# Second product of an MLP by Strassen's seven half-size products, in pairs of tiles, on one Trainium2 core

## Chip, core and metric

The program runs on one core of one Trainium2 chip. The metric is device time in microseconds (us), the median over runs of the whole program. The engines are named as in the profile: PE (matrix products), PEld (its weight loads), DVE (vector), ACT (scalar), POOL (general purpose; it also issues the loads of q, k, v and the weights), SP (issues the DMA transposes).

## What is computed

Inputs are q, k, v of shape 4 x 8 x 768 x 64 (batch, heads, positions, head size), a gain `g_ln` of 512, and two weight matrices. The reference, cut to what matters:

```python
gamma = 1.0 - 2.0 ** (-5.0 - np.arange(H))            # one decay per head
for t in range(S):
    state = gamma * state + outer(k[:, :, t], v[:, :, t])
    y[:, :, t] = scale * (q[:, :, t] @ state)
x = y with the 8 heads side by side                    # 4 x 768 x 512
xn = (x - mu) / np.sqrt(var + 1e-06) * g_ln            # per position, over 512
out = x + np.maximum(xn @ w_ch1, 0.0) @ w_ch2          # 512 -> 2048 -> 512
```

The output is 4 x 768 x 512 in fp32.

## The kernel before

**Tiles.** The 4 x 768 positions are 24 tiles of 128 positions. Tiles 0 to 3 are the first chunk of each of the four batches, tiles 4 to 23 the other five chunks of each batch, batch after batch. Products are in bf16 with fp32 sums in PSUM.

**Steps of a tile.** Each step is one short function, called by its name (line numbers are those of the profile):

- `k`, `q`, `v` (L334): POOL issues the loads, which turn fp32 into bf16. `gk`, `gq`, `gv` (L363): a one-element copy on POOL that waits for a load.
- `tr` (L377): SP issues a DMA transpose of q and k. `eq` (L383): DVE scales the transposed q into `trq`.
- `vis` (L392, L398), a *visit*: PE multiplies k by q for the tile, or from tile 8 on for a pair of tiles (8 and 9, 10 and 11, ... 22 and 23) into banks X0 to X3, and q by the state of the chunk before into banks Y0 and Y1.
- `am` (L405): DVE multiplies with the decay mask into `asb`, two instructions per tile. `py` (L420): PE adds `asb` times v in Y0 and Y1. Y then holds x of the tile.
- `vg` (L454): POOL scales v. `pd` (L462): PE adds k times the scaled v to the running state in bank PD. `pb` (L472): DVE writes the state out as bf16, two instructions.
- `bn` (L428, L429): DVE takes mean and variance. `xn` (L438): DVE makes (x - mean) times gain in bf16, two instructions. `xc` (L444): ACT copies x to `x_all`.
- `ex` (L492): for tiles 8 and later SP issues a DMA transpose of `xn` into `xnt`.
- `m` (L517): PE multiplies with the first weight matrix `w1`, in groups of 1, 2 or 4 tiles (128, 256 or 512 columns per instruction; groups 0 to 7 are tiles 0 to 7, groups 8 to 11 are tiles 8 to 15 in twos, groups 12 and 13 tiles 16 to 19 and 20 to 23). A call fills one bank with 512 columns. `r` (L528, L530): ACT, at times DVE, takes the positive part into `h1`, 128 x 16 x 512 for four tiles.
- `z` (L540): PE multiplies `h1` of one tile with the second weight matrix `w2`: 16 instructions of 512 columns, in four calls. For tile 23 they are cut into 384 and 128 columns.
- `sq` (L505, ACT) and `rs` (L510, DVE): one over the standard deviation, in `rstd`. Since it is positive, it is applied only at the end: `ad` (L547): DVE takes `z`'s result times `rstd` plus x into `osb` (fp32). `st` (L554): ACT issues the store.

**Order.** The order of all steps is a table of names written out in the file (`ORDER`, some 1,000 entries); each engine runs its own instructions strictly in that order, and waits by semaphores where it needs another engine's result. After a `/` a name has the engine or the PSUM banks: `r8_4/A`, `z8_0//M`. Between a tile's visit and its first product, and between its first and its second, the table puts work of other tiles.

## Time and profile before

| what | number |
|---|---|
| runs | 211.12, 211.79 and 214.57 us, median 211.79 |
| span of the profiled execution, first to last instruction | 208.5 us |
| granted PE clock | 1.000 |
| PE busy | 203.1 us in 2031 instructions |
| DVE busy | 126.0 us in 297 instructions |
| ACT busy | 76.8 us in 168 |
| POOL busy | 95.6 us in 145 |
| DMA | 27.11 MB in 109946 packets |

Of the profiled execution only the span is given; it is 3.3 us below the median of the runs. To read the profile: a row by line gives the operation, its output and inputs by the program's names, the shape, how often it occurs, the busy time of the group and the mean length of one in ns. Matmuls are pipelined, so one of them lasts longer than the distance to the next: the distance is read from the chain of work that ended last, where the length of a piece divided by its count is the pitch. In the timeline, `x2` means that neighbours on one line are merged, and the bracket says how long the engine was idle before and for whom. In a table of windows, the first number is the length of the stretch, then come the busy times of the engines, the granted clock, the DMA share (over 1 where packets of several queues wait at once) and GB/s.

### The profile page before, as it was taken

Reading aid. Unit: us, or ns where it says so; the run is one execution under the profiler, and the core shown is the slowest. Engines: PE = TensorE matmul, PEld = TensorE weight load, DVE = VectorE, ACT = ScalarE, POOL = GpSimd, SP = SyncE. Lnnn points to the kernel's source line nnn. Section 1 sums busy time; section 2 is a strip of 40 time slices with the busy share of each in tenths; the row PEclk is TensorE's granted clock in tenths of the full one; section 3 lists DMA queues with packets and bytes.
Section 4 is the critical chain, followed back from the end, with each engine's and each line's share of the span. In section 5 each row is a group of like instructions: output and inputs, shape, how many; then the busy total and the mean of one; then the engine's idle time right before and its main releaser. Section 6 shows DMA issues by size and latency. Waiting matters only on the chain.

```text
span 208.5 us, 4986 instructions
## 1 busy us (share of the span) xinstructions
PE 203.1 (97%) x2031; PEld 131.4 (63%) x2031; DVE 126.0 (60%) x297; ACT 76.8 (37%) x168; POOL 95.6 (46%) x145
## 2 busy tenths in 40 slices
PE   7999999999999999999999999999999999999994
PEld 3568999897558566676587686565545444444443
DVE  7687898696349858579695666888948303110023
ACT  6466644442400414415137124223372612346000
POOL 8997593793696788770687559300000000000000
PEclk9999999999999999999999999999999999999999
DMA  9999999999999999999999999965032400015005
GB/s 129 175 180 181 160 199 163 167 183 155 150 140 159 129 180 144 161 98 207 205 160 161 203 161 116 159 79 129 0 105 101 102 0 3 0 50 203 0 3 201
DMA packets 109946, 27.11 MB, mean 130 GB/s; under 512 B 102625, under 2 KB 106977, under 8 KB 109922
## 3 DMA queue, kind: packets, MB, share of 16 engines
q0 software_dynamic: 77024, 13.37, 84.9%
q1 hardware_dynamic: 28242, 6.85, 24.4%
q10 hardware_dynamic: 4656, 6.56, 9.6%
q8 instruction: 16, 0.26, 0.6%
q14 instruction: 8, 0.07, 0.1%
HBM read 27.30 MB, written 6.29 MB: 161 GB/s over the span
## 4 chain that ended last, share of the span: by engine, by line
PE 92%; DVE 4%; DMA 2%; issue 0%; ACTq 0%; ACT 0%; DVEq 0%
PE X L517 40%; PE M L540 27%; PE Y L540 10%; PE PD L540 4%; PE X L392 3%; PE Y L420 3%; PE PD L462 2%; DMA osb<-in_q_dram 2%; DVE asb L405 1%; PE Y L398 1%; DVE trq L383 1%; DVE xn L438 1%; DVE bns L428 1%; PE Y L369 1%; PE M L369 1%; PE X L325 1%
## 5 line engine op out<-in xcount | busy, mean ns | idle before, releaser
L517 PE MATMUL X<-xnt,w 128*128 128x128 bf16 (+2 forms) x896 | 93.8, 257 | 0.0
L528 ACT ACTIVATE h<-X 128x512 bf16<-128x512 f32 x89 | 51.2, 602 | 81.7 <-PE X L517 70.9
L517 PEld LDWEIGHTS <-w 128*128 128x128 bf16 x896 | 66.1, 98 | 20.5 <-issue 0.2
L540 PE MATMUL M<-w,h 128*128 128x512 bf16 x256 | 61.5, 379 | 0.0
L540 PEld LDWEIGHTS <-h 128*128 128x128 bf16 x400 | 37.4, 98 | 37.9
L405 DVE TENSOR_TENSOR asb<-X,mask 128x512 bf16<-128x512 f32 x48 | 30.5, 682 | 12.3 <-PE X L392 12.1
L454 POOL TENSOR_TENSOR vg<-v,vsc 128x512 bf16<-128x512 bf16 x20 | 21.2, 1062 | 7.9 <-DMA v<-in_v_dram 7.8
L547 DVE SCALAR_TENSOR_TENSOR osb<-M,rstd,x_all 128x512 f32<-128x512 f32 x16 | 11.9, 746 | 20.6 <-PE M L540 20.2
L334 POOL DMA_DIRECT2D v<-in_v_dram x24 | 21.8, 911 | 3.7 <-DMA w<-in_moe_w_ch_dram 2.0
L444 ACT CAST x_all<-Y 128x256 bf16<-128x256 f32 (+1 forms) x39 | 14.4, 411 | 24.7 <-DVE xn L438 24.7
L540 PE MATMUL Y<-w,h 128*128 128x512 bf16 (+1 forms) x96 | 21.8, 370 | 0.0
L428 DVE BATCH_NORM_STATS2 bns<-Y 128x6 f32<-128x256 f32 (+1 forms) x39 | 16.3, 453 | 8.5 <-PE Y L420 8.3
L438 DVE SCALAR_TENSOR_TENSOR xn<-Y,mv,gb 128x256 bf16<-128x256 f32 (+1 forms) x39 | 18.6, 512 | 1.2 <-PE Y L420 0.6
L472 DVE TENSOR_TENSOR state<-PD,gch 64x256 bf16<-64x256 f32 x40 | 16.6, 415 | 0.6 <-PE PD L462 0.3
L334 POOL DMA_DIRECT2D qk<-in_q_dram x17 | 15.2, 893 | 1.3 <-issue 1.3
L334 POOL DMA_DIRECT2D qk<-in_k_dram x17 | 15.3, 898 | 0.9 <-issue 0.7
L547 DVE SCALAR_TENSOR_TENSOR osb<-PD,rstd,x_all 128x512 f32<-128x512 f32 (+1 forms) x3 | 1.9, 617 | 20.1 <-PE PD L540 20.1
L383 DVE TENSOR_TENSOR trq<-tr,qsc 128x512 bf16<-128x512 bf16 x17 | 9.1, 537 | 3.5 <-DMA tr<-qk 3.3
L561 PE MATMUL PD<-zeros 128*128 128x512 bf16 (+1 forms) x33 | 8.5, 392 | 1.2 <-DVE zeros L247 1.2
L420 PEld LDWEIGHTS <-asb 128*128 128x128 bf16 x192 | 8.0, 98 | 2.6 <-DVE asb L405 0.7
L363 POOL COPY scrap<-qk 1x1 bf16<-1x1 bf16 x28 | 4.9, 177 | 9.7 <-DMA qk<-in_k_dram 8.5
L540 PE MATMUL PD<-w,h 128*128 128x512 bf16 (+1 forms) x48 | 8.8, 326 | 0.0
(75 smaller groups left out, 130.5 us busy)
## 6 DMA issues: line engine op xcount, KB each, us to landing
out_dram<-osb ACTq DMA_DIRECT2D x23, 256.0 KB, 2.4
w<-in_moe_w_ch_dram POOLq DMA_DIRECT2D x8, 512.0 KB, 8.4
v<-in_v_dram POOLq DMA_DIRECT2D x24, 128.0 KB, 6.5
qk<-in_k_dram POOLq DMA_DIRECT2D x17, 128.0 KB, 6.8
qk<-in_q_dram POOLq DMA_DIRECT2D x17, 128.0 KB, 5.1
k<-in_k_dram POOLq DMA_DIRECT2D x6, 128.0 KB, 7.6
q<-in_q_dram POOLq DMA_DIRECT2D x6, 128.0 KB, 7.4
tr<-qk SPq DMA_TRANSPOSE x17, 6.1
```

What stands on the lines that cost most here:

```text
L334: nc.gpsimd.dma_start(out=dst, in_=tok[kind][TILES[t]])
L405: nc.vector.tensor_tensor(out=slot(asb, t)[:, :, par, :], in0=bank(("pa", t, par)).rearrange("p (i t) -> p i t", t=P), in1=mask.rearrange( ...
L420: nc.tensor.matmul(dst, lhsT=slot(asb, t)[:, h // 2, h % 2, :], rhs=v_of(t)[:, h, :], start=(not late and n == H and h == 0), stop=(h >= H ...
L428: nc.vector.bn_stats(out=bns[:, t, i, :], in_=x)
L438: nc.vector.scalar_tensor_tensor(out=dst, in0=src, scalar=mv[:, t, 0:1], in1=g, op0=ALU.subtract, op1=ALU.mult)
L444: nc.scalar.copy(out=dst, in_=src)
L454: nc.gpsimd.tensor_tensor(out=slot(vgs, chunk(t)), in0=v_of(t), in1=vsc[:, c, :].unsqueeze(2).to_broadcast([P, H, D]), op=ALU.mult)
L472: nc.vector.tensor_tensor(out=slot(state, chunk(t) - 1)[o, :, o], in0=pd[o, :, o], in1=gch[o, c - 1, :].unsqueeze(2).to_broadcast([D, NPAI ...
L517: nc.tensor.matmul(bank(("mm", g, ho))[:, j * n * P:(j + 1) * n * P], lhsT=w1[:, ko, (ho + j) * P:(ho + j + 1) * P], rhs=x[:, x0:x0 + n, k ...
L528: nc.scalar.activation(out=dst, in_=src, func=AF.Relu)
L540: nc.tensor.matmul(bank(("m2", t, piece))[:, 0:hi - lo], lhsT=slot(h1, t // 4)[:, ho, t % 4 * P:(t % 4 + 1) * P], rhs=w2[:, ho, lo:hi], st ...
L547: nc.vector.scalar_tensor_tensor(out=slot(osb, t + piece)[:, 0:hi - lo], in0=bank(("m2", t, piece))[:, 0:hi - lo], scalar=rstd[:, t:t + 1] ...
```

## The change

For tiles 0 to 7 nothing changes except places in memory. For tiles 8 to 23 the second product is made for two tiles together, by Strassen's scheme. With h of tile t and of tile t+1 cut into halves along the 2048 (h(t,0), h(t,1)) and `w2` cut into four blocks W11, T3 (upper right), W21, W22 of 1024 x 256, a pair needs seven products of 8 instructions with 256 columns (`s`, L607), where the two tiles took 32 instructions with 512 columns.

- `tm` (L582): DVE makes four sums of blocks of `w2` once (T1 = T3 - W11, T2 = W22 + T1, T3 = W22 + T3 in place, T4 = W21 - T2), each 128 x 2048 in bf16. T1, T2 and T4 lie in a new tile `early`, which first holds q, k, v and transposed k of early tiles.
- `sa` (L596): DVE makes four differences of halves of h per pair, each 128 x 1024 in bf16 (S1, S2, S4 in three shared tiles `sum`; the third one in place in `h1`).
- `o` (L621): DVE puts the products and x together in `osb`, six instructions per pair: the first with 512 columns (two blocks at once), five with 256. Six of the seven products are summed by PE in the two halves of one bank (`sm`), which `o` reads in between; the seventh has a bank of its own (`sb`). `ad` is left for tiles 0 to 7 only.
- Products of two tiles can be mixed only if both are normalized. For tiles 8 to 23, `sr` (L564, ACT) and `rt` (L568, DVE) make `rstd` per tile right after `bn`; `xn` writes fp32 (into `arg` and `grow`, which are free by then); and a new step `xg` (L572, ACT) multiplies by `rstd` and writes the bf16 `xn` that `ex` transposes.
- `xnt` has 3 slots for 4; `osb` has 3 slots of two tiles for 6 of one. Tile 23 is no longer cut 384/128 at the end; its two halves of 256 columns are stored apart.
- The table `ORDER` is the same up to the visit of tiles 8 and 9, and new from there on.

The diff, cut to its core:

```diff
 ORDER = """
...
-z2_3 ad0 tr10 gq10 z3_0//M v12 gk11 st0/A ad2 z3_1 tr11 eq8 q13 vis8//X2,X1,X3,X0 z3_2 am8b am8a
-gv10 vg10/ gv11 z3_3 am9a am9b py8 m7_12//X1 bn8 m7_4//X3 ad3 q12 py9 pd9 bn9 gk12 k13 m6_4//X0
+z2_3 ad0 tr10 gq10 z3_0//M v12 gk11 st0/A ad2 z3_1 tr11 eq8 q13 vis8//X2,X1,X3,X0 tm1 z3_2 am8b am8a
+z3_3 q12 am9a py8 am9b m6_4//X1 gk12 vg10/ bn8 py9 m7_8//X0 k13 xc9b xc8b bn9 sq7 vg11/ m7_4//X2
...
+    early = sb.tile([P, 12, DM], BF16, name="early")
...
-    osb = slots("osb", [P, DM], FP32)
+    osb = slots("osb", [P, 2, DM], FP32)
+    sums = [sb.tile([P, HK, P], BF16, name=f"sum{i}") for i in range(3)]
+    xhat = [arg.rearrange("p i t -> p (i t)"), grow]
...
-        dst, src, g = y_parts(t, half, slot(xns, t))
+        dst, src, g = y_parts(t, half, slot(xns if t < S0 else xhat, t))
...
+    @on("sr")
+    def _(eng, t):
+        nc.scalar.activation(out=rstd[:, t:t + 1], in_=mv[:, t, 1:2], func=AF.Sqrt, bias=epsb, scale=1.0)
+
+    @on("rt")
+    def _(eng, t):
+        nc.vector.reciprocal(out=rstd[:, t:t + 1], in_=rstd[:, t:t + 1])
+
+    @on("xg")
+    def _(eng, t):
+        nc.scalar.activation(out=slot(xns, t), in_=slot(xhat, t), func=AF.Copy, scale=rstd[:, t:t + 1])
+
+    W11, W21, W22, T3 = w2[:, 0:HK, 0:HM], w2[:, HK:, 0:HM], w2[:, HK:, HM:], w2[:, 0:HK, HM:]
+    T1, T2, T4 = (early_b[:, i * HK:(i + 1) * HK] for i in range(3))
+    S1, S2, S4 = sums
+
+    @on("tm")
+    def _(eng, i):
+        out, in0, in1, op = {1: (T1, T3, W11, ALU.subtract), 2: (T2, W22, T1, ALU.add),
+                             3: (T3, W22, T3, ALU.add), 4: (T4, W21, T2, ALU.subtract)}[i]
+        nc.vector.tensor_tensor(out=out, in0=in0, in1=in1, op=op)
...
+    def left(t, i):
+        return {1: h_of(t, 0), 2: h_of(t, 1), 3: S4, 4: h_of(t + 1, 1), 5: S1, 6: S2, 7: h_of(t + 1, 0)}[i]
+
+    right = {1: W11, 2: W21, 3: W22, 4: T4, 5: T1, 6: T2, 7: T3}
+
+    @on("sa")
+    def _(eng, t, i):
+        out, in0, in1 = {1: (S1, h_of(t + 1, 0), h_of(t + 1, 1)), 2: (S2, h_of(t, 0), S1),
+                         3: (h_of(t + 1, 0), h_of(t + 1, 0), h_of(t, 0)), 4: (S4, h_of(t, 1), S2)}[i]
+        {"P": nc.gpsimd, "": nc.vector}[eng].tensor_tensor(out=out, in0=in0, in1=in1, op=ALU.subtract)
...
+    @on("s")
+    def _(eng, t, i):
+        for ho in range(HK):
+            nc.tensor.matmul(product(t, i), lhsT=left(t, i)[:, ho, :], rhs=right[i][:, ho, :],
+                             start=(ho == 0 and i in (1, 2)), stop=(ho == HK - 1), skip_group_check=True)
+
+    @on("o")
+    def _(eng, t, i):
...
+            n, s, j, add = {2: (0, low, 2, o), 3: (0, high, 6, x), 4: (0, high, 3, o), 5: (1, high, 7, o),
+                            6: (1, low, 4, x)}[i]
+            out, in0, in1 = o[:, n, s], product(t, j), add[:, n, s]
+        nc.vector.tensor_tensor(out=out, in0=in0, in1=in1, op=ALU.add)
```

**How the table moves instructions.** Three places follow; the numbers in the names are those of buffers.

DVE from the visit of tiles 12 and 13 to the means of the first of the two, before (`trq` is scaled q, `asb` the masked product, `osb` the output tile):

```order
L405 TENSOR_TENSOR asb0_146<-X2_63,mask_74 128x4x128
L405 TENSOR_TENSOR asb1_147<-X1_62,mask_74 128x4x128
L405 TENSOR_TENSOR asb1_147<-X0_61,mask_74 128x4x128
L405 TENSOR_TENSOR asb0_146<-X3_64,mask_74 128x4x128
L472 TENSOR_TENSOR state1_96<-PD_68,gch_81 64x4x64 x2
L547 SCALAR_TENSOR_TENSOR osb1_159<-M_67,rstd_90,x_all_94 128x512
L428 BN_STATS bns_88<-Y0_65 128x6
L428 BN_STATS bns_88<-Y1_66 128x6
L429 BN_AGGR mv_89<-bns_88 128x2
```

The same engine in the change, from the end of the normalization of tile 12 past the visit of tiles 14 and 15 (`arg` is one of the two fp32 tiles for normalized x, `h10` is `h1` of tiles 8 to 11, `sum0` is S1):

```order
L451 SCALAR_TENSOR_TENSOR arg_79<-Y0_65,mv_89,gb_87 128x4x64
L582 TENSOR_TENSOR early_98<-w2_93,early_98 128x2048
L596 TENSOR_TENSOR sum0_149<-h10_144 128x1024
L568 RECIPROCAL rstd_90<-rstd_90 128x1
L418 TENSOR_TENSOR asb1_136<-X2_63,mask_74 128x4x128
L418 TENSOR_TENSOR asb0_135<-X0_61,mask_74 128x4x128
L418 TENSOR_TENSOR asb0_135<-X1_62,mask_74 128x4x128
L418 TENSOR_TENSOR asb1_136<-X3_64,mask_74 128x4x128
L553 SCALAR_TENSOR_TENSOR osb0_146<-M_67,rstd_90,x_all_94 128x512
L582 TENSOR_TENSOR w2_93<-w2_93 128x8x256
L596 TENSOR_TENSOR sum1_150<-h10_144,sum0_149 128x1024
L441 BN_STATS bns_88<-Y0_65 128x6
```

Between a visit's four `asb` instructions and the steps around them now stand two sums of `w2` and two of h, which were nowhere before; the reciprocal of tile 13 stands ahead of the `asb` rows.

SP around the transposes of tiles 8 to 15, before (rows with `tr` are q and k of a tile, rows with `xnt` are normalized x; the first two are x of tiles 8 and 9, the next two q and k of tiles 12 and 13, then x of tiles 10 and 11, then q and k of tiles 14 and 15):

```order
L492 DMA_TRANSPOSE xnt2_154<-xn0_148 128x4x128
L492 DMA_TRANSPOSE xnt2_154<-xn1_149 128x4x128
L377 DMA_TRANSPOSE tr5_135<-qk5_127 128x8x128
L377 DMA_TRANSPOSE tr0_130<-qk6_128 128x8x128
L492 DMA_TRANSPOSE xnt2_154<-xn2_150 128x4x128
L492 DMA_TRANSPOSE xnt2_154<-xn3_151 128x4x128
L377 DMA_TRANSPOSE tr1_131<-qk7_129 128x8x128
L377 DMA_TRANSPOSE tr2_132<-qk0_122 128x8x128
```

The same in the change:

```order
L505 DMA_TRANSPOSE xnt2_143<-xn0_137 128x4x128
L505 DMA_TRANSPOSE xnt2_143<-xn1_138 128x4x128
L390 DMA_TRANSPOSE tr0_122<-qk6_120 128x8x128
L390 DMA_TRANSPOSE tr5_127<-qk5_119 128x8x128
L390 DMA_TRANSPOSE tr2_124<-qk0_114 128x8x128
L390 DMA_TRANSPOSE tr1_123<-qk7_121 128x8x128
L505 DMA_TRANSPOSE xnt2_143<-xn3_140 128x4x128
L505 DMA_TRANSPOSE xnt2_143<-xn2_139 128x4x128
```

Tiles 12 and 13 have changed places, and the transposes of q and k of tiles 14 and 15 now stand ahead of those of x of tiles 10 and 11.

The end of ACT's queue, the last stores, before:

```order
L554 DMA out_0_dram<-osb2_160 128x512
L554 DMA out_0_dram<-osb4_162 128x512
L554 DMA out_0_dram<-osb3_161 128x512
L554 DMA out_0_dram<-osb5_163 128x384
L554 DMA out_0_dram<-osb0_158 128x128
```

And in the change, from the store of tile 18 on:

```order
L560 DMA out_0_dram<-osb0_146 128x512 x2
L560 DMA out_0_dram<-osb1_147 128x512
L560 DMA out_0_dram<-osb2_148 128x256
L560 DMA out_0_dram<-osb2_148 128x512
L560 DMA out_0_dram<-osb1_147 128x512
L560 DMA out_0_dram<-osb2_148 128x256
```

Before, tiles 20, 22 and 21 and the two pieces of tile 23 were left for the end; in the change it is tiles 18, 19 and 20, one half of tile 23, tiles 22 and 21, and the other half of tile 23.

171 lines of the change are left out of this document (95 added, 76 removed).

## The prediction

> **What bounds the kernel now.** I read the page first: engines, slices, and the chain that ended last.
>
> ```profile
> span 208.5 us, 4986 instructions
> PE 203.1 (97%) x2031; PEld 131.4 (63%) x2031; DVE 126.0 (60%) x297; ACT 76.8 (37%) x168; POOL 95.6 (46%) x145
> PE   7999999999999999999999999999999999999994
> DVE  7687898696349858579695666888948303110023
> DMA  9999999999999999999999999965032400015005
> GB/s 129 175 180 181 160 199 163 167 183 155 150 140 159 129 180 144 161 98 207 205 160 161 203 161 116 159 79 129 0 105 101 102 0 3 0 50 203 0 3 201
> PE 92%; DVE 4%; DMA 2%; issue 0%; ACTq 0%; ACT 0%; DVEq 0%
> ```
>
> PE is busy in every slice but the first and the last, and the chain is 92% PE. DVE is full only until about two thirds of the span and then nearly idle. DMA is full for 25 of the 40 slices. A busy PE may still hide gaps, since matmuls are pipelined, so I took the pitch from the pieces of the chain:
>
> ```profile
> 105.97 1.75 PE X L517 x16
> 198.42 3.45 PE PD L540 x16
> 204.68 0.91 PE PD L540 x16
> 205.61 0.35 DVE osb L547
> ```
>
> Instructions of 512 columns follow each other at 3.45/16 = 0.216 us, those of 256 columns (groups 8 to 11 on L517) at 1.75/16 = 0.109 us, half of it. Pieces of L517 and L540 come at this pitch from about 20 us to the end, so PE has no gaps to give: only less PE work, or a shorter end, can make the program faster, and every new wait of PE is added to its time.
>
> **Term 1, PE work.** The change removes 16 tiles x 16 = 256 instructions of 512 columns: 256 x 0.216 = 55.2 us. It adds 8 pairs x 7 x 8 = 448 of 256 columns: 448 x 0.109 = 49.0 us. No other PE work changes. Term: -6.2 us. The new products load weights of the same size from the same kind of tile at the pace at which groups 8 to 11 already do.
>
> [...]
>
> **Term 2, the end.** Before, the last matmul runs to 205.6, then come one short DVE instruction (0.35 us), the store of a strip of 64 KB and the closing. Stores cannot go faster than this:
>
> ```profile
> 190.00:192.00 2.00, 2.00 (x11) 0.89 (x10) 0.00 (x0) 1.09 (x2) 0.00 (x0) 1.00 1.00 378
> 202.69 3.65 ACTq L554 DMA_DIRECT2D out_dram<-osb  x5
> out_dram<-osb ACTq DMA_DIRECT2D x23, 256.0 KB, 2.4
> out_dram<-osb ACTq DMA_DIRECT2D x1, 64.0 KB, 1.6
> ```
>
> With a DMA share of 1.00 they move 378 GB/s, 0.69 us for a tile of 256 KB. In the new order the stores of tiles 19, 20, 22, 21 and both halves of 23 are issued around the last three calls of PE: 4 x 256 + 2 x 128 KB = 1.3 MB, issued in about 2.3 us, which take 3.5 us to move. The last one is behind a queue of about 0.8 us, and the last DVE instruction has 256 columns for 128 (0.1 us more). Term: +0.9 us. Lower bound +0.2 (if the stores keep up, the wider last piece alone), upper +1.3 (if they start 0.4 us later than I count).
>
> **Term 3, DVE from the visit of tiles 8 and 9 to that of 22 and 23.** This is where the new work lies. Visit to visit, before:
>
> ```profile
> 61.50:74.70 13.20, 13.20 (x159) 8.70 (x160) 9.74 (x22) 3.62 (x10) 9.99 (x19) 1.00 1.96 154
> 74.70:88.00 13.30, 13.30 (x139) 9.22 (x140) 9.90 (x25) 4.93 (x12) 10.66 (x18) 1.00 1.58 156
> 88.00:101.10 13.10, 13.10 (x135) 9.01 (x136) 9.71 (x22) 4.76 (x11) 5.18 (x12) 1.00 1.76 169
> 101.10:115.90 14.80, 14.80 (x153) 10.93 (x152) 10.16 (x25) 6.36 (x13) 10.94 (x16) 1.00 1.63 172
> 115.90:132.50 16.60, 16.60 (x159) 11.37 (x160) 11.34 (x22) 5.72 (x13) 12.83 (x19) 1.00 1.57 164
> 132.50:143.60 11.10, 11.10 (x111) 6.75 (x110) 9.06 (x21) 3.06 (x8) 0.00 (x0) 1.00 0.87 108
> 143.60:155.80 12.20, 12.20 (x107) 6.27 (x108) 8.97 (x22) 5.56 (x12) 0.00 (x0) 1.00 0.28 66
> 155.80:205.40 49.60, 49.60 (x289) 23.98 (x288) 12.51 (x24) 14.30 (x29) 0.00 (x0) 1.00 0.18 63
> ```
>
> The first seven rows: 94.3 us of PE, 68.9 us of DVE. In the same stretch the new order has 32 calls of `z` fewer (18 for 50, 0.863 us each), 21 calls of `s` (0.875 us each) and one more of `m`: 94.3 - 27.6 + 18.4 + 0.9 = 86.0 us of PE. For DVE it has 4 `tm`, 15 `sa`, 16 `o` (3 of them wide), 13 `rt`, and 7 `ad` and 5 `rs` fewer. Their prices:
>
> ```profile
> L300 DVE TENSOR_TENSOR mask<-vsc,cm 128x1024 f32<-128x1024 f32 x1 | 1.2, 1224 | 0.1
> L276 DVE TENSOR_TENSOR arg<-fidx,lgq 128x512 f32<-128x512 f32 x1 | 0.7, 673 | 0.0
> L383 DVE TENSOR_TENSOR trq<-tr,qsc x17: 404/426/2181, 44.0 to 149.8; 128x512 bf16<-128x512 bf16 x17
> L472 DVE TENSOR_TENSOR state<-PD,gch 64x256 bf16<-64x256 f32 x40 | 16.6, 415 | 0.6 <-PE PD L462 0.3
> L547 DVE SCALAR_TENSOR_TENSOR osb<-M,rstd,x_all 128x512 f32<-128x512 f32 x16 | 11.9, 746 | 20.6 <-PE M L540 20.2
> L510 DVE RECIPROCAL rstd<-rstd 128x1 f32<-128x1 f32 x8 | 1.0, 141 | 0.0
> ```
>
> The two fp32 rows give 0.12 us fixed and 1.08 ns per element; the bf16 row (median 426) then 0.60 ns per element. An `sa` (1024 elements, all bf16) is an estimate of 0.73 us by the bf16 row, 1.22 by the fp32 row; a `tm` (2048) 1.34 or 2.33. I take the bf16 prices, the operands being of its kind. An `o` reads PSUM like `state`: 0.42 us, the wide one 0.67. Sum: 68.9 + 4 x 1.34 + 15 x 0.73 + 13 x 0.42 + 3 x 0.67 + 13 x 0.14 - 7 x 0.75 - 5 x 0.14 = 88.6 us. That overstates, since back to back an instruction starts before the one ahead ends:
>
> ```profile
> 88.42 2.48 DVE L405 TENSOR_TENSOR asb<-X,mask 128x512 bf16<-128x512 f32 x4 [2.40 <-PE X L392]
> 128.62 2.18 DVE L383 TENSOR_TENSOR trq<-tr,qsc 128x512 bf16<-128x512 bf16 x1
> 128.48 2.03 POOL L454 TENSOR_TENSOR vg<-v,vsc 128x512 bf16<-128x512 bf16 x2
> ```
>
> Four `asb` of 0.68 us take 2.48 us: 0.08 us less each. With 48 instructions added that is up to 3.8 us: 84.8 us of DVE against 86.0 of PE, where it was 69 against 94. DVE is 99 to 103% loaded in this stretch and becomes nearly a second bound; behind each late DVE instruction are queued the `asb` rows of the next visit, and PE waits for them in `py`. After the last visit DVE has 12.5 us plus 17 `sa`, 32 `o` less 10 `ad`, about 32 us against 51.6 of PE: no bound there.
>
> The other two rows show a collision: a DVE instruction with two SBUF inputs, begun during POOL's `vg`, lasted until the second `vg` had ended, 2.18 us for 0.43. The new `sa` and `tm` are of that kind, and 13 `vg` lie in the stretch. I take 0.9 us of new PE waits for DVE, between 0 (if all fits) and 3 (88.6 - 86.0 and a collision not hidden).
>
> **Term 4, DMA transposes.** Here `xg` is the added link: after `bn` the chain to `m` runs over ACT and DVE (`sr`, `rt`, `xg`) and then to SP.
>
> ```profile
> 69.20 2.52 SPq L492 DMA_TRANSPOSE xnt<-xn  x2
> 71.82 4.18 SPq L377 DMA_TRANSPOSE tr<-qk  x2
> DMA to landing us min/median/max: 3.0/6.1/9.2
> 74.67 0.62 PE L392 MATMUL X<-trq,tr 64*128 64x128 bf16 x16
> 76.56 1.91 PE L517 MATMUL X<-xnt,w 128*128 128x256 bf16 x16
> ```
>
> SP issues x of tiles 8 and 9 at 69.2 and 70.5, then q and k of tiles 12 and 13 at about 71.8 and 73.6. `xg` puts these some 1.1 us later: one ACT instruction of 0.6 and the `pb` that now stands ahead of `xn`. The first product of tiles 8 and 9, which PE began at 76.6, is due at about 77.6 in the new order; that fits. Between the visits of tiles 8 and 10, and of 10 and 12, the new table has six calls of `z` and four of `m` (5.2 and 3.5 us), a visit of 0.9 and about 1.1 of `py` and `pd`: 21.3 us. So the visit of tiles 12 and 13 is due at 82.8 where it was 88.0, 5.2 us earlier, while its transposes are issued later: 73.6 + 1.1 + 1.4 of issue + 6.1 to land (the median for `tr`) + 0.4 for `trq` gives 82.6 us, with a spread of 3 us either way by the same row. As DMA is full there, I take 0.9 us; bounds 0 and 3.5. Next in SP's queue stand q and k of tiles 14 and 15, which wait for their loads, ahead of x of tiles 10 and 11; the same lateness passes on, rather than being paid again. Later loads have time, since the last visits come 8 us earlier, but the loads of tiles 21 to 23 stand at least 7 us of PE earlier in the table. `xg` itself costs ACT 16 x 0.6 us of idle time it has (ACT is 37% busy); if it were the bound, that would be 9.6 us.
>
> **Sum.** 208.5 - 6.2 + 0.9 + 0.9 + 0.9 = 205.0 us of span, 3.5 us less. The median of the runs, 211.79, is 3.3 us above the span; taken off that, 208.3 us.
>
> **Rivals.**
>
> - *Clean.* DVE and DMA keep up; new waits stay under 1.1 us in sum. For it: the prices of term 3 are upper ones, and PE had no gap after 20 us before. Against it: the loads of 99% on DVE and full DMA together. -6.2 + 0.9 + 0.3: 206.8 us, and faster by over 2% wherever waits stay under 1.1. Chance 0.34.
> - *DMA holds the visits.* The three intervals after the first pair's visit shrink from 39.6 to 32.5 us of PE while their DMA share is already 1.58 to 1.96. If loads and transposes cannot go faster, PE waits most of the 7.1 us; with 1.6 of it as slack, 5.5: -6.2 + 0.9 + 5.5 = +0.2, 212.0 us. Against it: GB/s there (154 to 169) is under the 203 to 207 of other slices. Chance 0.12.
> - *DVE holds PE, slower than before.* If `sa` and `tm` run at the fp32 price, they cost 15 x 0.49 + 4 x 0.99 = 11.3 us more, DVE has 96 to 100 us in a stretch of 86, and PE waits 10 to 14: -6.2 + 0.9 + 11.5 = +6.2, 218.0 us. It decides once DVE's work there passes 95 us. Chance 0.09. [...]
> - *Half-width matmuls do not pay half.* If the fixed part of an instruction were not hidden in the new stream, lengths would count instead of pitches:
>
> ```profile
> L540 PE MATMUL M<-w,h 128*128 128x512 bf16 x256 | 61.5, 379 | 0.0
> L517 PE MATMUL X<-xnt,w 128*128 128x256 bf16 x256 | 31.5, 273 | 0.0
> ```
>
> 273/379 is 0.72, so 448 x 0.216 x 0.72 = 69.7 us, 14.5 us more instead of 6.2 less: +14.5 + 0.9 + 1.8 = +17.2, 229.0 us. It decides from a pitch of 55.2/448 = 0.123 us on; against it stands the pitch of 0.109. Chance 0.02. [...]
>
> **How the numbers follow.** Two per cent of 211.79 is 4.2 us, about what a measurement of this kernel can tell from no change. The forecast case (waits of 1.1 to 5 us) has 0.43, "clean" 0.34, DMA 0.12, DVE 0.09, the split 0.02. Faster: 0.34. Within 2%: 0.43 + 0.12 = 0.55. Slower: 0.11. The range goes from the full gain with the smallest end, 211.79 - 6.2 + 0.2 = 205.8, to the upper bounds of terms 2 to 4 taken together, -6.2 + 1.3 + 3.0 + 3.5 = +1.6, 213.4.
>
> **What would show it.** In the new profile the chain should have L607 in pieces of 8 at 0.875 us (term 1 is wrong if they are longer). DVE should be busy 84 to 89 us between the visits of 8 and 22, with `sa` near 0.7 and `tm` near 1.3 us; at 1.2 and 2.3 the slow rival holds. Gaps of PE before L405 that end at `trq` or `tr` are term 4, gaps before L433 or L607 that end on DVE are term 3; none at all means "clean". The last store should land about 0.9 us later behind the last matmul than before. A PE gap at a place not named here, above 2 us, would make the prediction wrong in kind.

## The result, and the profile after

| kernel | median of the runs, us | range | ratio to before, 95% interval |
|---|---|---|---|
| before | 211.45 | 210.57 to 214.57 | |
| changed | 220.21 | 219.51 to 221.72 | 1.0434, 1.0382 to 1.0486 |

The changed kernel is slower by 4.3%; 208.3 us was forecast, and at most 213.4. Times are medians of all runs, while the ratios leave out the slower executions (over 1.5% above the fastest) that most of the kernels have, so that two kernels are better compared by their ratios. The profiled execution has a span of 217.7 us where it had 208.5. From its page (PEclk is the granted clock of PE, slice by slice):

```profile
span 217.7 us, 5442 instructions
PE 201.6 (93%) x2207; PEld 151.1 (69%) x2207; DVE 158.0 (73%) x374; ACT 88.4 (41%) x194; POOL 98.2 (45%) x145
PE   7999999999999878478899999999999999999992
DVE  7687797693398977825878999989997656014971
PEclk9999999999999999959999999999999999999999
DMA  9999999999999999999999799993101020421016
DMA 35%; PE 30%; POOL 26%; issue 7%; DVE 1%; POOLq 0%; DVEq 0%
```

PE, which had no gap, is thinner from the 14th to the 20th slice (5.4 us each, so 71 to 109 us), and in the 18th its clock is about half. The chain is no longer PE's: it runs over DMA and POOL. DVE, which term 3 saw loaded to 99% between the visits, holds 1% of it.

By stages (columns as in the windows of the prediction; the first two rows are stretches between visits, the third from the visit of tiles 8 and 9 to that of 22 and 23, the last from there to the last product):

```profile
61.76:73.62 11.86, 11.12 (x150) 7.81 (x149) 11.15 (x27) 5.32 (x14) 8.87 (x12) 1.00 1.98 181
86.58:105.95 19.37, 13.92 (x125) 9.65 (x126) 11.77 (x26) 5.50 (x14) 8.18 (x15) 0.82 1.57 150
61.76:161.54 99.78, 90.20 (x989) 68.28 (x989) 83.02 (x195) 43.60 (x102) 52.01 (x82) 0.97 1.31 133
161.54:213.20 51.66, 51.66 (x421) 37.48 (x420) 29.63 (x66) 16.36 (x33) 0.00 (x0) 1.00 0.17 52
```

Between these two visits the kernel before took 94.3 us, all PE work. I had counted 86.0 us of work for the new one; it took 99.8. So 13.8 us were lost there. Behind the last visit it took 51.7 us, free of gaps. The whole difference of the spans, 9.2 us, is +5.5 between the visits, +2.1 behind them (the new table has products left over there), +1.4 at the end and +0.2 ahead.

PE's waits in the stretch (the timeline of PE; in brackets the idle time ahead of the row and what ended it):

```profile
78.38 0.38 PE L475 MATMUL PD<-vg,k 128*128 128x128 bf16 x4 [0.99 <-POOL vg L467]
86.58 0.62 PE L405 MATMUL X<-trq,tr 64*128 64x128 bf16 x16 [0.77 <-DVE trq L396]
93.85 0.58 PE L475 MATMUL PD<-vg,qk 128*128 128x128 bf16 x4 [4.57 <-POOL vg L467]
101.49 2.79 PE L530 MATMUL X<-xnt,w 128*128 128x256 bf16 x24 [0.88 <-DMA xnt<-xn]
107.54 0.38 PE L475 MATMUL PD<-vg,qk 128*128 128x128 bf16 x4 [0.74 <-POOL vg L467]
```

The largest is not at a place that the prediction names: `pd14` waits 4.57 us for `vg14`, the scaled v of tile 14, on POOL. The timeline of POOL around it, after:

```profile
79.33 0.87 POOL L347 DMA_DIRECT2D v<-in_v_dram  x1
81.92 1.78 POOL L347 DMA_DIRECT2D v<-in_v_dram  x2
91.00 0.41 POOL L376 COPY scrap<-v 1x1 bf16<-1x1 bf16 x2 [2.93 <-DMA v<-in_v_dram]
91.85 0.87 POOL L347 DMA_DIRECT2D v<-in_v_dram  x1 [0.44 <-issue]
92.74 1.05 POOL L467 TENSOR_TENSOR vg<-v,vsc 128x512 bf16<-128x512 bf16 x1
99.00 0.18 POOL L376 COPY scrap<-qk 1x1 bf16<-1x1 bf16 x1 [5.09 <-DMA qk<-in_q_dram]
101.61 0.30 POOL L376 COPY scrap<-v 1x1 bf16<-1x1 bf16 x1 [2.44 <-DMA v<-in_v_dram]
106.46 1.03 POOL L467 TENSOR_TENSOR vg<-v,vsc 128x512 bf16<-128x512 bf16 x1
```

and before:

```profile
74.26 0.94 POOL L334 DMA_DIRECT2D v<-in_v_dram  x1
80.27 0.89 POOL L334 DMA_DIRECT2D v<-in_v_dram  x1
81.67 1.04 POOL L454 TENSOR_TENSOR vg<-v,vsc 128x512 bf16<-128x512 bf16 x1 [0.35 <-DMA v<-in_v_dram]
84.83 1.11 POOL L454 TENSOR_TENSOR vg<-v,vsc 128x512 bf16<-128x512 bf16 x1 [1.24 <-DMA v<-in_v_dram]
```

Before, the loads of v of tiles 14 and 15 went out at 74.26 and 80.27 and `vg14` ran at 81.67, `vg15` at 84.83. After, they go out at 79.33 and 91.85, and `vg14` runs at 92.74, `vg15` at 106.46, though the prediction has 7.1 us less PE work ahead of their visit. Around these two POOL now issues q, k and v of tiles 18 and 19: q of 18 and k of 19 ahead of 79.33, the other four behind it, the two loads of v at 81.92 among them; that visit begins at 135. And its one-element copies wait for just these loads: at 91.00 for v of tile 18 (2.93 us), at 99.00 for q of tile 19 (5.09 us). What stands behind these copies in POOL's row starts later too: the load of v of tile 15 at 91.85, `vg14` at 92.74.

One number I had not looked for is the clock. Behind the wait of 4.57 us (windows of after; the clock is the last but two):

```profile
91.00:94.00 3.00, 0.15 (x2) 0.15 (x2) 0.51 (x1) 0.00 (x0) 2.40 (x5) 0.68 1.60 157
94.00:98.00 4.00, 4.00 (x28) 3.01 (x27) 1.26 (x4) 0.00 (x0) 0.00 (x0) 0.50 1.89 162
98.00:99.00 1.00, 1.00 (x7) 0.68 (x6) 0.00 (x0) 0.60 (x1) 0.00 (x1) 0.55 1.60 167
99.00:101.00 2.00, 1.62 (x21) 1.22 (x19) 0.81 (x3) 1.15 (x3) 0.17 (x1) 1.00 0.73 81
```

From 94 to 99 us PE works at about half speed: 4 x 0.50 + 1 x 0.45 = 2.5 us more on top of the wait.

### The profile page after: what moved, and what is told of

It is laid out like the page before. It is cut to its first block, busy times and chain, and to the rows that moved or that the text cites. A ratio compares the mean times of both kernels' runs of the same rounds, so it can differ in the third digit from the quotient of the medians.

```text
span 217.7 us, 5442 instructions
## 1 busy us (share of the span) xinstructions
PE 201.6 (93%) x2207; PEld 151.1 (69%) x2207; DVE 158.0 (73%) x374; ACT 88.4 (41%) x194; POOL 98.2 (45%) x145
## 4 chain that ended last, share of the span: by engine, by line
DMA 35%; PE 30%; POOL 26%; issue 7%; DVE 1%; POOLq 0%; DVEq 0%
DMA v<-in_v_dram 17%; PE X L530 10%; POOL qk L347 9%; DMA qk<-in_k_dram 7%; POOL vg L467 5%; PE PD L607 5%; PE Y L607 5%; PE M L607 4%; DMA w<-in_moe_w_ch_dram 4%; POOL v L347 4%; DMA qk<-in_q_dram 3%; POOL scrap L376 3%; POOL early L347 2%; PE X L607 2%; DMA tr<-qk 2%
## 5 line engine op out<-in xcount | busy, mean ns | idle before, releaser
L530 PE MATMUL X<-xnt,w 128*128 128x128 bf16 (+2 forms) x872 | 90.0, 257 | 0.9 <-DMA xnt<-xn 0.9
L541 ACT ACTIVATE h<-X 128x512 bf16<-128x512 f32 x83 | 47.4, 600 | 56.7 <-PE X L530 51.7
L607 PEld LDWEIGHTS <-h 128*128 128x128 bf16 x256 | 24.6, 98 | 4.1
L467 POOL TENSOR_TENSOR vg<-v,vsc 128x512 bf16<-128x512 bf16 x19 | 19.8, 1045 | 9.4 <-DMA v<-in_v_dram 9.3
L548 PE MATMUL M<-w,h 128*128 128x512 bf16 x96 | 23.1, 380 | 0.0
L347 POOL DMA_DIRECT2D v<-in_v_dram x23 | 20.6, 899 | 3.3 <-DMA w<-in_moe_w_ch_dram 2.0
L607 PEld LDWEIGHTS <-sum 128*128 128x128 bf16 x192 | 18.4, 98 | 3.0 <-issue 0.2
L376 POOL COPY scrap<-qk 1x1 bf16<-1x1 bf16 x28 | 6.7, 238 | 12.7 <-DMA qk<-in_q_dram 8.4
L596 DVE TENSOR_TENSOR sum<-h,sum 128x1024 bf16<-128x1024 bf16 x16 | 11.0, 685 | 1.4 <-PE Y L607 1.3
L475 PE MATMUL PD<-vg,qk 128*128 128x128 bf16 x52 | 5.2, 225 | 6.1 <-POOL vg L467 6.0
L433 PE MATMUL Y<-v,asb 128*128 128x64 bf16 x176 | 9.2, 195 | 0.3
```

The lines of the kernel that those rows point to most:

```text
L347: nc.gpsimd.dma_start(out=dst, in_=tok[kind][TILES[t]])
L376: nc.gpsimd.tensor_copy(out=scrap, in_=old[0:1, 0, 0:1])
L433: nc.tensor.matmul(dst, lhsT=slot(asb, t)[:, h // 2, h % 2, :], rhs=v_of(t)[:, h, :], start=(not late and n == H and h == 0), stop=(h >= H ...
L467: nc.gpsimd.tensor_tensor(out=slot(vgs, chunk(t)), in0=v_of(t), in1=vsc[:, c, :].unsqueeze(2).to_broadcast([P, H, D]), op=ALU.mult)
L530: nc.tensor.matmul(bank(("mm", g, ho))[:, j * n * P:(j + 1) * n * P], lhsT=w1[:, ko, (ho + j) * P:(ho + j + 1) * P], rhs=x[:, x0:x0 + n, k ...
L541: nc.scalar.activation(out=dst, in_=src, func=AF.Relu)
```

## The experiments

Three questions, in this order. What makes the waits: L (the loads of tiles 18 and 19, issued early, slow those that are due), G (only POOL's copies that wait for them) or D (DVE's work)? When the queues are in order, what is left: P (the pace of the transfers) or Q (the order of queues)? And do the seven products pay at all: A (yes, as counted) or B (no)? Where a kernel changes only the table, the diff shows the names that moved.

### vg14 ahead

```diff
-... gk17 gv18 xg10 gv14 tm2 v15 vis12//X0,X1,X2,X3 st1/A ex10/S z6_2 vg14/ pb14 ...
+... vg14/ gk17 gv18 xg10 gv14 tm2 v15 vis12//X0,X1,X2,X3 st1/A ex10/S z6_2 pb14 ...
```

> One step of POOL is moved: the scaling of v for tile 14 (vg14) stands ahead of the one-element copies gk17, gv18 and gv14 instead of behind them; nothing else changes. In the changed kernel PE waited 4.7 us at 88.9 for this step, and ran at half clock from about 92.5 to 98.7 behind the wait. Theory L (the loads of tiles 18 and 19, issued long ahead of need, fill the DMA queues, so that v of tiles 14 and 15 lands late): the wait at pd14 falls under 1 us, but v of tile 15 still lands at about 101 and vg15 still runs at about 106, so that PE now waits some 6 to 9 us at pd15 for it: the time stays within 2 us of the changed kernel's, 218 to 221 us. Theory G (only the place of vg14 behind the copies matters): wait and half clock go, 4.7 + 2.7 us, and nothing replaces them: 212 to 214 us. Theory D (DVE is the bound in this stretch): no change beyond 2 us and no new wait at pd15; PE waits for DVE instead.

221.4 us, ratio 1.0473 (1.0391 to 1.0556). The wait at `pd14` is gone and comes back one step later:

```profile
97.30 0.59 PE L430 MATMUL Y<-v,asb 128*128 128x64 bf16 x8 [4.44 <-DMA v<-in_v_dram]
101.48 5.27 PE L527 MATMUL X<-xnt,w 128*128 128x256 bf16 x24 [1.88 <-DMA xnt<-xn]
```

Now `py13` waits for v of tile 13 itself, whose load stands ahead of these copies in POOL's row, but behind the loads of v of tiles 18 and 19. That speaks against G: data are late, not only the instruction behind the copies. L has the time about right, but not the place: it had the wait at `pd15`.

### The copies further back

```diff
-... gk17 gv18 xg10 gv14 ... gq21 am12a gq19 gv15 v16 ... s8_5 pb16 ...
+... gk17 xg10 gv14 ... gq21 am12a gv15 v16 ... s8_5 gv18 gq19 pb16 ...
```

> Two one-element copies on POOL that wait for loads (gv18 and gq19, for v of tile 18 and q of tile 19) are moved back, behind pd15's POOL work; the loads themselves stay where they are. POOL then no longer stands still for 2.9 us at 88 and 5.1 us at 94. Theory G (the waiting copies alone hold POOL): vg14 and vg15 run early, the waits at pd14 and pd15 fall under 1 us each and the half clock goes: 211 to 213 us. Theory L (the loads of tiles 18 and 19 fill the DMA queues): vg14 runs some 2 to 3 us earlier, but v of tile 15 still lands at 98 to 101 behind the loads of 18 and 19, the copy gv15 waits for it, and PE waits 4 us or more at pd15: 216 to 219 us. Theory D (DVE is the bound): 218 us or more, with PE waiting for DVE.

223.74 us, ratio 1.0528 (1.0482 to 1.0574): no better. With the copies out of the way the loads still come late:

```profile
98.45 0.59 PE L430 MATMUL Y<-v,asb 128*128 128x64 bf16 x8 [4.79 <-DMA v<-in_v_dram]
```

It is v of tile 13 again. G falls; L has its time (216 to 219 us) too low and its wait at another place.

### The loads of tiles 18 and 19 when they are due

```diff
-... xn9a q18 z4_2 ... am10a k19 pd12 ... q17 bn10 ... v18 ... v19 ... k18 ... q19 ...
-... tr19 ... tr18 vg15/ ... k21 ... q22 ... vg16/ ...
+... vg16/ q18 k18 k19 q19 v18 v19 k21 q22 ...
+... tr19 tr18 tr16 ... gv18 gq19 gv19 gk19 vg19/ ...
```

> The loads of q, k, v of tiles 18 and 19 (and k of 21, q of 22) go behind vg16, that is behind the loads of tiles 13 to 16 that are needed sooner; the copies that wait for them and gv15 go back accordingly, and the DMA transposes of tiles 18 and 19 go behind those of x of tiles 12 and 13. Nothing else changes. Theory L: v of tiles 14 and 15 lands at about 84 to 88 and 92, no wait of PE at pd14 or pd15 over 1 us, no half clock, so that about 5.6 us of waits and 2.7 us of half clock go: 210 to 213 us; what is left over the 205 us predicted are the waits at the visits of tiles 10 and 12. Theory G: the same as for the copies alone, 211 to 213 us. Theory D (DVE is the bound): the waits move to DVE results and the time stays at 216 us or more.

218.52 us, ratio 1.0385 (1.0349 to 1.0421). The waits for `vg14` and `vg15` fall to 0.28 us and nothing, as L has it. The time (210 to 213 by L) hardly falls, because another queue now shows (timelines of PE and SP):

```profile
97.61 4.09 PE L527 MATMUL X<-xnt,w 128*128 128x256 bf16 x24 [3.89 <-DMA xnt<-xn]
85.62 4.36 SPq L387 DMA_TRANSPOSE tr<-qk  x2
90.08 2.54 SPq L502 DMA_TRANSPOSE xnt<-xn  x2
```

On SP the transposes of x of tiles 10 and 11 stand behind those of q and k of tiles 14 and 15; they go out only at 90.08, when these have been issued. The prediction saw this row of the queue and held its lateness to be paid for already.

### The end, and the early stores

Two kernels that leave stores out, to size term 2 and to see whether the stores of tiles 0 to 5 take DMA time from the loads.

```diff
-... s20_4 st19/A o22_5 st20/A o22_2 ...
+... s20_4 o22_5 o22_2 ...
```

> The changed kernel without the stores of tiles 19 and 20 (these 512 KB of the output are left out). In the changed kernel the span ends 4.5 us behind the last matmul, 1.4 us more than before, and the DMA share is 1.0 from 213 to 216. If the queue of the last stores sets the end (term 2 of the prediction), 512 KB less at some 375 GB/s take 1.4 us off the queue, and with the issue of two stores gone the last store lands as early as in the kernel before: 1.0 to 1.6 us less, 218.6 to 219.2 us. If the end is set by something else (the wider last DVE instruction, the closing), under 0.4 us less.

220.13 us (1.042, 1.0366 to 1.0473). In its profile the end behind the last product is 3.8 us for 4.5, so the queue of the last stores may hold some 0.7 us of it, half of what was expected; in the runs that is too little to be told from nothing.

```diff
-st0/A ... st1/A ... st2/A ... st3/A ... st4/A ... st5/A
```

> The changed kernel without the stores of tiles 0 to 5 (these 1.5 MB of the output are left out), all else as it is. They are issued between about 60 and 107 us, where the DMA engines are full. Theory P (pace: between the visits of tiles 8 and 16 the DMA engines cannot move a pair's loads, transposes and stores as fast as the new table asks for them): six stores of about 0.7 us of all engines, 4 us of traffic, are gone, v of tile 15 and the transposes land 2 to 4 us earlier, and the waits of PE between 70 and 108 fall by 2 to 4 us: 216 to 218.5 us. Theory Q (queue order: loads and waiting copies of tiles 18 and 19 stand ahead of what is needed sooner on POOL, transposes of q and k ahead of those of x on SP): the order on the queues is the same, so are the waits: 219.5 us or more.

220.5 us (1.042, 1.0348 to 1.0492): nothing gained, as Q has it. As long as the queues are out of order, 1.5 MB less on the DMA engines does not help.

### All queues in the order in which things are due

```diff
+... v15 gk17 xg10 tm2 vis12//X0,X1,X2,X3 st1/A ex10/S tr15 tr14 z6_2 gv14 vg14/ ...
+... vg16/ v17 q18 k18 k19 q19 v18 v19 k21 q22 ...
+... tr16 ... tr17 tr18 tr19 ... gv18 gq19 gv19 gk19 gv12 vg19/ ...
```

(on top of the kernel with the loads when they are due; the plus rows are the new places.)

> As e3_loads_due, and the rest of POOL's and SP's order put by need: on SP x of tiles 10 and 11 ahead of q and k of tiles 14 and 15, and q and k of 16 and 17 ahead of those of 18 and 19; on POOL v of tiles 15 and 17 earlier, and the copies that wait for a load just issued (gk12, gv12, gv14) behind the work they held up. PE, DVE and ACT keep their order. Theory Q: the 4.1 us wait of PE for x of tiles 10 and 11 at 93 and the 3.1 us at 119 to 126 of e3_loads_due fall under 1 us each: 210 to 213 us. Theory P: the waits are paid at other places in the same stretch (at visits, at m or at pd), 3 us or more of them in all between 70 and 125: 215 us or more.

216.29 us, ratio 1.0237 (1.017 to 1.0304), and in the profiled execution no clock below full. Order alone gives back nearly half of the loss, and the wait for x of tiles 10 and 11 is gone, as Q has it. But the number is P's (215 or more): other waits of PE, the longest 2.25, 1.52 and 1.19 us, stand in the same stretch. What the first two wait for follows below. And without the stores of tiles 0 to 5:

> e6_queues_due without the stores of tiles 0 to 5 (left out of the output), to see what pace is left as a limit once the queues are in order. Theory P: 2 to 4 us less than e6_queues_due. Theory Q: within 1 us of it.

214.48 us, ratio 1.0103 (1.0063 to 1.0142): by the ratios 1.3% or 2.8 us less, which is P's number (2 to 4 us), where leaving out the same stores gave nothing before. So P has a part, once the queues no longer hide it. The same kernel, and DVE relieved of the 16 differences of tiles 8 to 15 by

```diff
-        return {... 3: S4, ... 5: S1, 6: S2, ...}[i]
+        s1, s2, s4 = (S1, S2, S4) if t >= 16 else (h_of(t, 0),) * 3
+        return {... 3: s4, ... 5: s1, 6: s2, ...}[i]
```

> The kernel with its queues in due order and without the stores of tiles 0 to 5 (214.48 us), and without the 16 differences of h on DVE for tiles 8 to 15 as well: their products take plain h, so the output of tiles 8 to 15 is not the reference's, and that of tiles 0 to 5 is not stored. DVE has 16 x 0.69 = 11 us less in the stretch from the visit of tiles 10 to that of 22. Theory D (DVE, loaded to 99%, is what still holds PE): the 5 us of waits between 77 and 117 us go, 209.5 to 210.5 us. Theory P (the pace of loads and transposes holds it, DVE only at one place): only the wait of 1.69 us for the sum and perhaps the 0.5 behind it go, 212.3 to 213 us.

212.6 us, ratio 1.0043 (1.0001 to 1.0085): by the ratios 0.6% or 1.3 us less for 11 us less DVE work, and the two intervals overlap. That is theory P's number (212.3 to 213), not D's.

### eq18, eq14 and eq15 behind what is due sooner

In the kernel with all queues in order, DVE itself stood still (timelines of DVE and PE):

```profile
112.45 0.42 DVE L393 TENSOR_TENSOR trq<-tr,qsc 128x512 bf16<-128x512 bf16 x1 [4.96 <-DMA tr<-qk]
116.68 1.05 PE L604 MATMUL M<-w,sum 128*128 128x256 bf16 x8 [1.52 <-DVE sum L593]
```

`eq18` waited 4.96 us for a transpose that I had moved back, with the sums of tiles 8 and 9 behind it.

```diff
-... m10_12//X1 eq18 sr14 ... ex14/S eq19 gk14 ...
+... m10_12//X1 sr14 ... ex14/S eq19 eq18 gk14 ...
```

> The kernel with its queues in due order (216.29 us) with one more step moved: the scaling of tile 18's q (eq18) stands behind that of tile 19, where it stood ahead of the sums of tiles 8 and 9. In that run's trace DVE waited 4.96 us there for the transpose of q and k of tile 18, which I had moved back, and behind it stood the sums and reads that PE waited 1.68 us for. Theory D2 (DVE's queue order, not DVE's amount of work, makes the 1.68 us and what follows): 1.5 to 2.5 us faster, 213.8 to 214.8 us. Theory D (DVE's amount of work): the wait comes back elsewhere, 215.5 to 216.5 us.

214.0 us, ratio 1.0117 (1.0069 to 1.0164): D2's number. The next place shows the same pattern:

```profile
93.78 0.42 DVE L393 TENSOR_TENSOR trq<-tr,qsc 128x512 bf16<-128x512 bf16 x1 [4.24 <-DMA tr<-qk]
96.07 1.87 PE L527 MATMUL X<-xnt,w 128*128 128x256 bf16 x8 [3.50 <-ACT h L538]
```

`eq15` waits 4.24 us; behind it stand the norm of tile 12 and the means of tile 13, behind these ACT's copy, behind that ACT's `r`, and for that PE waits 3.50 us and runs at half clock afterwards (0.50 from 96 to 100 us).

```diff
-... vg15/ eq15 xc13b ... r8_6/A eq14 r8_12/A ... xn12a z7_1 ...
+... vg15/ xc13b ... r8_6/A r8_12/A ... xn12a eq15 eq14 z7_1 ...
```

> All eight pairs, queues in due order, eq18 late (214.00 us), and now the scaling of q of tiles 14 and 15 (eq14, eq15) right ahead of their own visit, where they stood ahead of the means and the norm of tiles 12 and 13. Theory Q (what holds PE is steps of DVE that stand in its queue ahead of steps that are due sooner, and wait for a transfer): the 3.67 us wait at 92 us and the half clock behind it (0.50 over 4 us, 0.76 over 4 us, some 2.5 us) go, a later visit of tile 14 may take 1 us back: 208 to 210 us, ratio 0.983 to 0.993. Theory P (transfers themselves are too slow for the shortened stretch, whatever waits for them): PE waits as long at the visit of tiles 14 and 15 itself, 213 to 214.5 us.

212.63 us, ratio 1.0026 (0.9989 to 1.0064). Q's direction, but between its 208 to 210 and P's 213 to 214.5. The waits that are left are many and small: PE's timeline marks seven between the two visits, none above 0.8 us, 3.0 us in sum. The whole stretch:

```profile
61.93:154.11 92.18, 88.25 (x984) 66.98 (x990) 84.06 (x195) 43.65 (x102) 52.07 (x82) 1.00 1.47 145
```

Between the two visits it takes 92.2 us, against 99.8 in the changed kernel, 94.3 before, and 86.0 counted. DVE is busy 84.1 of them, which may be why late steps are felt here; no run shows it. How those 6 us divide between DVE's load, the pace of the transfers and what is left of the order is open.

### Half of the pairs

The first four pairs alone (tiles 8 to 15), the changed kernel otherwise:

```diff
-        dst, src, g = y_parts(t, half, slot(xns if t < S0 else xhat, t))
+        dst, src, g = y_parts(t, half, slot(xhat if S0 <= t < 16 else xns, t))
...
-s16_1//Y0 xg23 sa16_1 s18_1//Y1 ex23/S sa16_2 s16_5 ...
+... tm5 ... z16_0//Y0 o12_6 ex23/S z17_0//Y1 z16_1 z16_2 ...
```

> The changed kernel with seven products for eight only for tiles 8 to 15; tiles 16 to 23 are normalized late and get z, as before (the block W12 that tm 3 overwrote is taken back by one more DVE instruction, and the end is not cut for tile 23). Theory A (the loss lies in the stretch of tiles 8 to 15): all the new waits of the changed kernel stay (some 11 us and 2.7 us of half clock), and the 3.2 us that the last four pairs gave are missing, the end some 0.5 us shorter: 221 to 223 us, ratio 1.045 to 1.055. Theory B (the scheme loses in every pair alike): half of the loss, 216 us, ratio 1.02.

222.7 us, ratio 1.0451 (1.0381 to 1.0522): A, at the edge of its range. This kernel has the queues of the changed kernel, and with them its waits (4.55 us for `vg14` among them). So it shows where the loss lies, not what the first four pairs would give in a better order. And the last four pairs alone, on the table of before (the first two lines are against the code of the changed kernel, the last two against the table of before):

```diff
- 'S0': 8,
+ 'S0': 16,
...
-z16_0//PD am23a am22a m12_8//X1 ...
+... s16_1//PD m12_15//X0 ... s18_1//M r12_14/A r12_12/A r12_9/A sa16_1 s16_2//Y0 ...
```

> The kernel before with its own table up to the visit of tiles 20 and 21, and seven products for eight only for the last four pairs (tiles 16 to 23), whose loads are all in SBUF by then; tiles 8 to 15 keep z. Theory A (the products pay as counted, and the loss of the changed kernel comes from new PE waits in the stretch in which the loads of q, k, v still run): PE work 8 x 16 x 0.216 - 4 x 7 x 8 x 0.109 = 3.2 us less, the end 0 to 1 us longer, no new PE wait above 0.6 us: 208.3 to 209.3 us, ratio 0.985 to 0.99. Theory B (the scheme itself loses: its sums on DVE, its reads of PSUM between products, its longer end): half of the loss of the changed kernel, 211.45 + 4.4 = 216 us, ratio 1.02, with waits of PE on sum or on osb in the tail.

223.09 us, ratio 1.0555 (1.0506 to 1.0605). That is beyond both theories. In the trace (DVE, then PE) the loss is waits again, this time of my own order of the tail:

```profile
119.42 2.64 DVE L576 TENSOR_TENSOR early<-w 128x2048 bf16<-128x2048 bf16 x1
146.94 3.63 PE L542 MATMUL M<-w,h 128*128 128x512 bf16 x16 [1.46 <-ACT h L535]
213.16 1.03 PE L601 MATMUL PD<-w,h 128*128 128x256 bf16 x8 [1.51 <-DVE osb L615]
```

A `tm` of 1.22 us lasts 2.64 beside POOL's `vg` (POOL is busy for all of 118 to 121 us), ahead of `asb`; an `r` stands behind `xg` on ACT; a product stands behind the `o` that reads its bank. So the experiment had not told A from B, and the order had to be put right first.

```diff
-... vis20//X1,X2,X0,X3 ad14 pd21 am21a z15_0//M z15_1 eq22 ...
+... vis20//X1,X2,X0,X3 tm1 tm2 ad14 am21a am20b st11/A pd21 m12_4//M am21b ...
```

> The same as the run with the last four pairs only (223.09 us), with its steps from the visit of tile 16 on put in another order: its trace showed PE waits of 14.3 us there for steps that my order put too late (m behind the r that empties its bank, 0.85 to 0.95 us each; a tm during POOL's vg, 2.64 us, ahead of asb; r behind xg on ACT, 1.62 us; products behind the o that reads their bank, 0.68 to 1.67 us). Here tm comes after the last vg, each o and sa has another pair's product or an m to cover it, and no step is dropped. Theory A (the seven products pay as counted once DVE's and ACT's steps are covered; no load runs here any more): 211.5 - 3.2 = 208.3 us with an end about as before, up to 209.3 with an end 1 us longer; ratio 0.985 to 0.99, no PE wait above 0.5 us after the visit of tile 16. Theory B (the scheme itself loses, whatever the order): still 214 us or more, with waits of PE on sum, osb or h.

214.25 us, ratio 1.0112 (1.0062 to 1.0161). 9 us from order alone, and PE's timeline still marks 3.3 us of waits behind the visit of tile 16. (In this kernel and the next, the table lends bank PD to `z12` while it holds the running sum of the last batch, so that their attention state there is not the reference's; the steps are the same in number and size.) The same with six pairs:

```diff
- 'S0': 16,
+ 'S0': 12,
```

> The run with the last four pairs in its rearranged order, extended to six pairs (tiles 12 to 23), whose second products come after the visit of tile 18; the order is rearranged from the visit of tile 12 on, the order of loads, gates, vg and transposes of q and k on POOL and SP is that of the kernel before. Theory A: 12 x 16 x 0.216 - 6 x 7 x 8 x 0.109 = 4.8 us of PE work less, 206.7 to 208 us, ratio 0.978 to 0.985, if visits that come earlier than before do not meet their loads; a wait of PE for vg or trq between 88 and 135 us takes it back, at most to what the four pairs give. Theory B: 214 us or more.

224.79 us, ratio 1.0615 (1.0549 to 1.0681). A failed again: its PE waits ahead of a `pd` until DVE has written the state out (1.6 us at 98 us), for x (1.9 at 108) and at the visit of tiles 18 and 19 for `trq` and for ACT's `r` (1.1 and 1.7), in the stretch where loads still run, and more behind. How much of it is the order and how much the loads was not taken further.

With PD left alone and a new order:

```diff
-z12_0//PD ...
+z12_0//M ...
```

> The last four pairs only, again with its steps from the visit of tile 16 on in another order: PD keeps the running sum until the last visit, and the order now counts with three things that the two runs before showed: ACT's and DVE's reads of one PSUM bank follow each other in the order of the table, an xg takes ACT 0.72 us, and an x lands 2.4 to 4 us after its issue. Theory A (the seven products pay as counted once no step of DVE, ACT or SP is late): PE work 3.2 us less, the end up to 0.7 us longer: 208.3 to 209.2 us, ratio 0.985 to 0.99, PE waits behind the visit of tile 16 below 1 us in all. Theory B (the scheme loses in any order): as the runs before, 214 us or more.

213.97 us, ratio 1.0101 (1.0055 to 1.0147). A missed again; two waits of PE make 3 us, and both end on DVE. The larger (DVE, then PE):

```profile
179.63 0.69 DVE L615 TENSOR_TENSOR osb<-M,x_all 128x512 f32<-128x512 f32 x1 [3.77 <-DMA out_dram<-osb]
180.37 1.03 PE L601 MATMUL M<-early,sum 128*128 128x256 bf16 x8 [2.05 <-DVE osb L615]
```

The tile `osb` that `o18_1` fills was still being stored: its store stood late in ACT's row. So:

```diff
-... m13_14//X0 st13/A o16_2 o18_1 sa18_3 ...
+... m13_7//Y0 st13/A o16_2 s18_5 m13_13//Y1 r13_7/A m13_8//X3 o18_1 ...
```

(the part of the new order that is about this wait: three calls of PE now stand between the store of tile 13 and `o18_1`.)

> The last four pairs only (213.97 us), with its steps from the visit of tile 16 on in one more order, which now counts with a store's 2.2 us until its osb is free and with the collision of vg and two-input DVE steps; no step is dropped. Theory A (the seven products pay as counted): the 4.9 us of PE waits behind the visit of tile 16 go down to below 1 us, 211.5 - 3.2 = 208.3 to 209.5 us, ratio 0.985 to 0.99. Theory B (the scheme loses in any order): 213 us or more again, with waits at new places.

208.98 us, ratio 0.9875 (0.9842 to 0.9908): faster than before by 1.3%, with an interval clear of 1, though less than the 2% that the prediction counts as a change; and what A had asked for from the start. From its page:

```profile
span 206.5 us, 5182 instructions
PE   7899999999999999999999999899999999999993
PE 89%; DVE 6%; DMA 2%; issue 1%; ACT 1%; ACTq 0%; DVEq 0%
```

and from the visit of tiles 16 and 17 to the last product, this kernel and then the one before:

```profile
116.12:203.20 87.08, 85.84 (x730) 56.89 (x736) 62.06 (x130) 34.65 (x75) 12.83 (x19) 1.00 0.54 85
```

```profile
115.92:205.40 89.48, 89.48 (x657) 48.37 (x656) 41.88 (x89) 28.64 (x62) 12.83 (x19) 1.00 0.54 88
```

The chain is PE's again; 2.4 us of the 3.2 are there, for 20 us more DVE work (62.1 for 41.9) that is hidden. B falls, for these four pairs. That the four kernels with the last four pairs, all with the same steps, ran from 223.1 to 209.0 us shows what the order alone is worth.

## Why the prediction was wrong

```profile
L607 PE MATMUL M<-w,h 128*128 128x256 bf16 x64 | 8.3, 273 | 0.0
L596 DVE TENSOR_TENSOR sum<-h,sum 128x1024 bf16<-128x1024 bf16 x16 | 11.0, 685 | 1.4 <-PE Y L607 1.3
L582 DVE TENSOR_TENSOR early<-w,early 128x2048 bf16<-128x2048 bf16 x2 | 2.4, 1216 | 0.0
```

**Term 1** was right: the new products follow each other at 109 ns, each lasting 273 ns as the half-wide ones before, and the kernel whose waits are gone shows the gain (ratio 0.9875). The rival of half-width matmuls that do not pay half is refuted.

**Term 3** was right in its prices: `sa` 0.685 us (0.73 estimated), `tm` 1.22 (1.34), DVE busy 83.0 us between the visits (84.8 to 88.6), all a little under what was counted. Of PE's waits there only 1.4 us end on DVE (0.77 and 0.61 ahead of two visits), and the `trq` of the first of these had itself waited for a transpose. The rival "DVE holds PE" is refuted as the cause of the 9 us: moving steps with DVE's work unchanged brought the ratio from 1.0434 to 1.0026, and 11 us less of its work brought 0.6% in the kernel with queues in order.

**Term 2** was a little small: the end grew by 1.4 us, not 0.9, just over its bound of 1.3. The last stores move at full rate until 216 us:

```profile
213.00:214.00 1.00, 0.39 (x4) 0.10 (x2) 0.42 (x1) 0.00 (x0) 0.00 (x0) 1.00 1.01 368
215.00:216.00 1.00, 0.00 (x0) 0.00 (x0) 0.00 (x0) 0.00 (x0) 0.00 (x0) 1.00 0.95 352
```

**Term 4** is the step that failed. Its own number came out where it was worked out, but by luck: the visit of tiles 12 and 13 waits 0.94 us from one instruction to the next (0.9 taken), and both sides of that wait were late.

```profile
86.01 0.43 DVE L396 TENSOR_TENSOR trq<-tr,qsc 128x512 bf16<-128x512 bf16 x1 [1.36 <-DMA tr<-qk]
```

The last `trq` ends at 86.4, not 82.6: its transpose, issued at 75.7, took 10.3 us to land where 6.1 were taken, the median of all 17; the two at this place took 8.5 and 8.8 us in the kernel before. PE too came 2.8 us later than counted, at 85.6 for 82.8, after waits of 0.61 us at the visit before and 0.99 us for a `vg`, among others. What made the loss are two sentences behind that number. "Later loads have time, since the last visits come 8 us earlier, but the loads of tiles 21 to 23 stand at least 7 us of PE earlier in the table" looks at PE's row alone. On POOL's row the six loads of tiles 18 and 19 had been moved forward by 5 to 29 us (four of them by 26 to 29), past the loads of v of tiles 13, 14 and 15 and past `vg14` and `vg15`, which are due before them; POOL's row was never walked through, though POOL issues every load. And "the same lateness passes on, rather than being paid again" is wrong for SP: x of tiles 10 and 11 behind q and k of tiles 14 and 15 cost 0.88 us in the changed kernel and 3.89 once POOL was in order. So of the 13.8 us lost between the visits some 11 were new waits and 2.5 the half clock behind the longest, where term 4 had 3.5 at most.

The rival "DMA holds the visits" named the right kind, late transfers, and priced it too low (at most 7.1 us of waits): it took the loads as limited by their rate, where their order was the larger part. With the queues put in order step by step the same work took 216.29, then 214.0, then 212.63 us (ratios 1.0237, 1.0117, 1.0026); some 2.8 us went with the stores of tiles 0 to 5, so the rate has a part too. The prediction's own mark for being wrong in kind, "a PE gap at a place not named here, above 2 us", is what `pd14` shows.

What the runs do not settle: why the last 6 us between the visits of tiles 8 and 22 do not go when all eight pairs use the scheme, and with them the gain of 3.5 us that was forecast.

## What to carry to other kernels

When a table of instructions is written anew, walk each queue that issues transfers or waits for them, POOL's, SP's and also DVE's and ACT's, and ask of each entry what stands behind it that is due sooner. A wait cost here not its own step but everything behind it in the row: the 4.24 us of `eq15`, which was due only later, reached PE as 3.50. And a saving of work on the bounding engine is worth its count only where what feeds that engine comes as much earlier: here the last four pairs, whose loads were in, gave 1.3% once their steps were in a good order. The first four gave a loss with the queues of the changed kernel; whether a better order would make them pay was not tried alone, and all eight in the best order found here came out even.
